# A mixture-of-experts kernel on one core: eight experts run straight through, and only TensorE asks for their sizes

## The chip, the cores and the metric

The kernel runs on one core of one Trainium2 chip. The metric is the device time of one execution in microseconds (us). Three runs of the kernel before gave 909.44, 908.67 and 904.90 us, a median of 908.67 us. In the profile the engines are TensorE (PE for its matrix products, PEld for its loads of a stationary operand), VectorE (DVE), ScalarE (ACT), GpSimd (POOL) and SyncE (SP), which issues most of the transfers. A name with q behind it (POOLq, SPq, PEq) is the engine's sequencer, which reads the program and hands work to the engine.

## What is computed

Three parts in a row, all in float32:

```python
# attention over a window of 64 keys: 4 batches, 8 heads, 576 positions, 64 per head
attn = softmax(where(0 <= i - j < 64, q @ k.T / 8, -1e9)) @ v
x = attn.transpose(0, 2, 1, 3).reshape(2304, 512)
# dense: w_in 512 x 2048, w_out 2048 x 512
x = (relu(x @ w_in) ** 2) @ w_out
# routed: 8 experts, w1 512 x 1024, w2 1024 x 512; each token goes to one expert
logits = x @ w_gate
e = argmax(logits);  g = softmax(logits)[e]
out[token] = g * (relu(x[token] @ w1[e]) @ w2[e])
```

How many of the 2304 tokens fall to an expert is known only when the program runs.

## The kernel before

Each float32 operand of a product is kept as a rounded high half and the remainder (names ending in h and l), and a product is made of three matrix products: high by high, high by low, low by high (`mm3`, L165 to L168). Attention and the dense part run interleaved, 256 tokens at a time, and take the first 540 us. Their order is not touched by the change.

**Before the routed part.** When most tokens are routed, the expert with the most tokens so far is picked, and its first two tiles of 128 tokens are run early (expert number -1, `group_of` from L989), beside the end of the gate. For each token the gate writes its number and its weight into a table in memory (`tab_d`), which is read back as `tab`, expert by expert; the number of tokens left for each expert is in `cnt`.

**The routed part** (L1067 to L1072) goes through the experts 0 to 7 in turn. At an expert, every one of the five engines reads the expert's size from `cnt` into a register (L992) and goes down a tree of comparisons (`either`, L1051) to one of eleven copies of the expert's program, made for 128, 192, 256, 288, 320, ... 512 tokens (`SIZES`, L1065). At the end of that copy it jumps behind all of them. `arm` (L997) is one such copy:

- for up to 128 tokens, `tile_of` (L680): the tokens are the stationary operand, 512 hidden columns stream at once, and the hidden values are transposed again for the second product.
- for more, `group_of` (L728): for each of 8 blocks of 128 hidden columns, `up` streams all the tokens through 4 x 3 products, `relu` (L744) splits the result into halves (ACT the high half, DVE the low half), and `down` multiplies the block before with 512 columns of w2, tile by tile, into the banks `ys`. A last tile of at most 64 tokens puts its two halves side by side (L758 to L761).
- between the blocks the next expert is prepared: `split` (L277) turns an eighth of its weights into halves (two casts on ACT, two subtractions on DVE or POOL by the letters of `TILES`) and starts the load of a further eighth into a ring of seven buffers; `gather_tile` (L927) fetches 128 tokens' rows by POOL; `tokens_in` (L930) transposes them on TensorE and splits them into halves. Only the next expert's first two tiles are brought in ahead; its third and fourth at its own start (L1024).
- `scatter` (L789) scales a tile of results on DVE and writes it to the rows of `out` by POOL. An expert's last tile is scattered only when its copy has been left (L1070), from a buffer of its own.

Expert sizes over 512 would run a loop (`more`, L1039).

The order of the instructions on each engine is that of the code in the routed part (`manual_schedule`, L1067); before it, a scheduler orders DVE, POOL and SP.

Of the kernel before, what the change touches and what calls it, by code (L numbers as in the profile page):

```python
# [11 lines left out]
F32 = mybir.dt.float32  # L12
# [37 lines left out]
def kernel(  # L50
# [26 lines left out]
    SPLIT_AT = {1: (0, 1), 3: (2, 3), 5: (4, 5, 6, 7)}  # L77
# [3 lines left out]
    TILES = "a" * 16, "vvvp" * 4  # L81
    TILE = "vvaaaaavaaaaavaa", "vvvppvvppvvpvppp"
# [33 lines left out]
    nc.vector.memset(zero, 0.0)  # L116
    mask = bpool.tile([P, 2, P], F32, tag="mask", name="mask")
# [26 lines left out]
    cnt = cpool.tile([1, E], I32, tag="cnt", name="cnt")  # L144

# [522 lines left out]
    def early_tokens(t):  # L668
        ps = transposed(early["x"][t]).rearrange("p (k t) -> p k t", k=KD)
        halves(*(x[:, :, ST + t * P:ST + t * P + P] for x in xhl), ps)  # L670
# [52 lines left out]
    def half_tile(n):  # L723
        m = n % P
        return m if m <= P // 2 and n > P else 0


    def group_of(e, n, c0, ys, new_g, between, first=None):  # L728

        h1, l1, h2, l2 = wsp[e]  # L730
        T = -(-n // P)
        m = half_tile(n)
        hid = {}

        def up(f, a, m, ks=range(KD)):

            if f not in hid:
                hid[f] = psum("h", 2)
            xh, xl = (x[:, :, c0 + a:c0 + a + m] for x in xhl)
            for kk in ks:  # L740
                b_ = slice(kk * F1 + f * P, kk * F1 + f * P + P)
                mm3(hid[f][:, a:a + m], h1[:, b_], l1[:, b_], xh[:, kk, :], xl[:, kk, :], kk == 0, kk == KD - 1)

        def relu(f):  # L744
            h, l = new_g()
            ps = hid[f]
            nc.scalar.activation(h[:, :n], ps[:, :n], ACTF.Relu)  # L747
            for o, a in ((l[:, :n - m], slice(n - m)), (h[:, n:n + m], slice(n - m, n)))[:1 + (m > 0)]:
                nc.vector.scalar_tensor_tensor(  # L749
                    out=o, in0=ps[:, a], scalar=0.0, in1=h[:, a].bitcast(F32), op0=ALU.max, op1=ALU.subtract  # L750
                )
            hid[f] = h, l

        def down(f, ts=range(T)):
            gh, gl = hid[f]
            b_ = slice(f * DM, f * DM + DM)
            for t in ts:
                if m and t == T - 1:  # L758
                    a = slice(n - m, n + m)
                    nc.tensor.matmul(ys[t][:2 * m, :], lhsT=gh[:, a], rhs=h2[:, b_], start=f == 0, stop=False)  # L760
                    nc.tensor.matmul(ys[t][:2 * m, :], lhsT=gh[:, a], rhs=l2[:, b_], start=False, stop=f == 7)  # L761
                else:
                    a = slice(t * P, min(t * P + P, n))
                    mm3(ys[t][:a.stop - a.start, :], gh[:, a], gl[:, a], h2[:, b_], l2[:, b_], f == 0, f == 7)

        ts = [T - 1, *range(T - 1)] if m else range(T)
        for f in range(8):
            if f == 0 and T > 2:
                up(f, 0, 2 * P)
                up(f, 2 * P, n - 2 * P)  # L770
            elif f == 0 and first:
                up(f, 0, n, range(KD // 2))
                first()
                up(f, 0, n, range(KD // 2, KD))
            else:
                up(f, 0, n)
            relu(f)
            if f == 7:
                between(f)
            if f:  # L780
                down(f - 1, ts if f < 7 else ts[:2])
            if f < 7:
                between(f)
        down(7, ts[1::-1] if m else ts[:2])
        for t in ts[2:]:
            down(6, (t,))
            down(7, (t,))
# [142 lines left out]
    def tokens_in(t, m=P, x=None, ps=None):  # L930

        if x is None:
            x = xg[t]
        ps = transposed(x, ps).rearrange("p (k t) -> p k t", k=KD)[:, :, :m]
        halves(*(x[:, :, t * P:t * P + m] for x in xhl), ps)
# [16 lines left out]
    def between(f):  # L952
# [3 lines left out]
        if f == 1:  # L956
# [4 lines left out]
            count(cnt, ps)  # L961
            nc.sync.dma_start(tab, tab_d.rearrange("(p r) c -> p r c", p=P))
        if f == 2:
# [4 lines left out]
            early["r"] = rpool.tile([P, 4 * P], F32, tag="r", name="r")  # L968
            early["ylast"] = rpool.tile([P, DM], F32, tag="ylast", name="ylast")
# [19 lines left out]
    group_of(-1, 2 * P, ST, ybanks[2:], new_g, between, first)  # L989
# [5 lines left out]
    rpool, ylast = early["pool"], early["ylast"]  # L995

    def arm(e, n):  # L997

        T = -(-n // P)
        ys = ybanks[:T - 1] + ybanks[3:]  # L1000
        m = half_tile(n)
        if m:
            ys[T - 2], ys[T - 1] = ys[T - 1], ys[T - 2]
        col = e * KMAX

        def between(j):
            if j == 1 and e + 1 < E:
                for k in (2, 3):
                    gather_tile(e + 1, k)
            if j == (4 if T == 1 else 7) and e + 1 < E:  # L1010
                for k in range(2):
                    tokens_in(k, ps=ybanks[k] if T == 1 else None)
                    if e + 2 < E:
                        gather_tile(e + 2, k)
            for i in SPLIT_AT.get(j, ()) if T == 1 else (j,):
                if e + 1 < E:
                    split(e + 1, i, TILE if T == 1 else TILES)

        nc.vector.tensor_copy(lasts[e % 2], tab[:, col + T - 1 - (m > 0), :])  # L1019
        if T == 1:  # L1020
            tile_of(e, 0, ys[0], lambda: early["r"], new_g, between)
        else:
            for t in range(2, T):
                tokens_in(t, min(P, n - t * P))  # L1024
            group_of(e, n, 0, ys, new_g, between)
            T -= m > 0
            for t in range(min(m > 0, T - 1)):
                scatter(ys[t], tab[:, col + t, :], new_r())
            if m:
                y, r = ys[T], new_r()  # L1030
                nc.scalar.copy(r[:m, :], y[m:2 * m, :])
                nc.vector.tensor_tensor(r[:m, :], r[:m, :], y[:m, :], op=ALU.add)
                ent = tab[:m, col + T, :]
                nc.vector.tensor_scalar_mul(r[:m, :], r[:m, :], ent[:, 1:2].bitcast(F32))
                scatter(None, ent, r[:m, :])
            for t in range(m > 0, T - 1):
                scatter(ys[t], tab[:, col + t, :], new_r())

    def more(e, n):  # L1039

        with tc.For_i(4, (n + (P - 1)) // P, 1) as i:
# [5 lines left out]
            tokens_in(2, x=x)  # L1047
# [3 lines left out]
    def either(e, n, sizes):  # L1051

        if len(sizes) == 1:
            arm(e, sizes[0])
            if sizes[0] == 4 * P:
                with tc.If(n > 4 * P):
                    more(e, n)
# [55 lines left out]
```

## Time and profile before

| | |
|---|---|
| median of three runs | 908.67 us (904.90 to 909.44) |
| the profiled execution | 912.93 us |
| its span, from the first to the last instruction | 911.2 us |
| TensorE: products, share of the span | 782.2 us, 86% |
| DVE, ACT, POOL busy | 546.9, 362.8, 311.5 us |
| TensorE's mean granted clock | 0.937 of full speed |

The span runs from 0 to 911.2 us. The early two tiles' last product ends at 578.7 us; there the routed part begins. A product's time in the timeline overlaps the next product's, so the price of one in a row of them is the distance of two starts. The granted clock is given as a share of 2.4 GHz: 0.50 means 1.2 GHz. "issue" in a wait means that the engine waited for nothing the profile shows, as its sequencer had not handed on the next instruction.

### The profile page before, as it was taken

To read this page: it belongs to the slowest core of one execution; us is meant where nothing else is said; L and a number is where in the kernel's file an instruction comes from. 1 tells how busy PE (TensorE), PEld (TensorE's weight loads), DVE (VectorE), ACT (ScalarE), POOL (GpSimd) and SP (SyncE) were. 2 spreads that over 40 slices of the span, in tenths; PEclk is the share of its full clock that TensorE was granted. 3 is DMA by queue.
4 is the path that set the end of the run, shared out by engine and by line. 5 is a ranking of instruction groups with operands and counts; after the bars stand their busy time and mean duration, and the time that the engine had idled before them with its cause. 6 is when DMAs were issued, how large, how long until landed. Compare 5 with 4: busy or idle time off the path is not lost.

```text
span 911.2 us, 14100 instructions
## 1 busy us (share of the span) xinstructions
PE 782.2 (86%) x4995; PEld 680.8 (75%) x4995; DVE 546.9 (60%) x1262; ACT 362.8 (40%) x985; POOL 311.5 (34%) x307
## 2 busy tenths in 40 slices
PE   6977778999999999999999979369446869979795
PEld 5866667888888898888889968258335858868684
DVE  6999995884956648485674966554256243423312
ACT  6845553444444434444443444144134233322200
POOL 5767784122121312222210242553355231221201
PEclk9998999999999999999999999778777698989998
DMA  9635442211202111111110353555365452330101
GB/s 287 224 121 174 140 152 80 71 35 47 68 28 70 47 53 48 41 53 42 59 36 12 123 191 128 191 156 176 116 200 163 145 169 89 119 107 1 46 1 42
DMA packets 49870, 92.24 MB, mean 101 GB/s; under 512 B 7148, under 2 KB 23532, under 8 KB 49680
## 3 DMA queue, kind: packets, MB, share of 16 engines
q1 hardware_dynamic: 44688, 80.43, 27.5%
q0 software_dynamic: 4992, 9.62, 3.4%
q8 instruction: 78, 1.28, 0.7%
q14 instruction: 112, 0.92, 0.4%
HBM read 84.59 MB, written 10.21 MB: 104 GB/s over the span
## 4 chain that ended last, share of the span: by engine, by line
PE 68%; DVE 14%; issue 11%; DMA 3%; ACT 2%; SPq 1%; DVEq 0%; another core or an unknown queue 0%; POOLq 0%; ACTq 0%; POOL 0%
PE h L166 11%; PE h L167 11%; PE h L168 11%; PE y L168 9%; PE y L167 9%; PE y L166 9%; DVE tmp L205 2%; PE a L355 2%; DVE tmp L201 2%; DVE gl L471 2%; DVE tmp L209 2%; PE a L428 2%; PE a L676 2%; DMA vf<-in_v 1%; PE a L413 1%
## 5 line engine op out<-in xcount | busy, mean ns | idle before, releaser
L166 PE MATMUL h<-xh,w 128*128 128x256 f32 (+4 forms) x784 | 241.1, 308 | 9.5 <-DVE last L1019 8.1
L168 PE MATMUL h<-xh,w 128*128 128x256 f32 (+4 forms) x784 | 234.5, 299 | 1.2 <-POOL w L227 1.2
L167 PE MATMUL h<-xl,w 128*128 128x256 f32 (+4 forms) x784 | 235.0, 300 | 0.1
L166 PEld LDWEIGHTS h<-xh,w 128*128 128x128 f32 x784 | 154.8, 198 | 20.5 <-issue 8.5
L167 PEld LDWEIGHTS h<-xl,w 128*128 128x128 f32 x784 | 155.1, 198 | 7.3 <-DVE xl L163 0.5
L168 PEld LDWEIGHTS h<-xh,w 128*128 128x128 f32 x784 | 154.5, 197 | 3.9 <-POOL w L227 1.4
L168 PE MATMUL y<-w,gl 128*128 128x512 f32 x294 | 115.3, 409 | 25.1 <-DVE gl L471 25.1
L457 ACT ACTIVATE r<-h 128x256 f32<-128x256 f32 x144 | 55.3, 384 | 189.3 <-PE h L168 174.2
L166 PE MATMUL y<-w,gh 128*128 128x512 f32 x294 | 117.3, 399 | 0.8 <-ACT gh L464 0.6
L167 PE MATMUL y<-w,gh 128*128 128x512 f32 x294 | 116.5, 396 | 0.0
L466 DVE TENSOR_TENSOR r<-r 128x256 f32<-128x256 f32 x112 | 54.8, 489 | 72.5 <-ACT gh L464 63.5
L749 DVE SCALAR_TENSOR_TENSOR ggl<-h,ggh 128x256 fp32r<-128x256 f32 (+2 forms) x45 | 23.1, 513 | 119.5 <-ACT ggh L747 117.9
L541 DVE SCALAR_TENSOR_TENSOR tmp<-tmp,stg 128x512 f32<-128x512 f32 x128 | 91.4, 714 | 0.7
L275 POOL TENSOR_TENSOR w<-stg,w 128x512 fp32r<-128x512 f32 x35 | 45.9, 1324 | 133.4 <-ACT w L274 115.3
L329 POOL COPY q<-qd 64x256 f32<-64x256 f32 x56 | 46.0, 822 | 126.5 <-PE a L355 121.1
L471 DVE TENSOR_TENSOR gl<-r,gh 128x256 fp32r<-128x256 f32 x144 | 78.0, 542 | 14.7 <-POOL r L466 10.8
L168 PEld LDWEIGHTS y<-w,gl 128*128 128x128 f32 x294 | 53.8, 190 | 40.5 <-DVE gl L471 30.1
L747 ACT ACTIVATE ggh<-h 128x448 fp32r<-128x448 f32 (+3 forms) x45 | 21.6, 480 | 131.8 <-PE h L168 92.5
L166 PEld LDWEIGHTS y<-w,gh 128*128 128x128 f32 x294 | 55.8, 190 | 8.6 <-ACT gh L464 1.4
L464 ACT ACTIVATE gh<-r 128x256 fp32r<-128x256 f32 x144 | 60.0, 418 | 3.7
L227 POOL TENSOR_TENSOR w<-tmp,w 128x512 fp32r<-128x512 f32 x32 | 52.5, 1645 | 24.7 <-ACT w L226 24.5
L407 POOL TENSOR_TENSOR s<-s,tot 128x512 f32<-128x512 f32 x28 | 30.8, 1099 | 88.4 <-DVE tot L406 33.4
(179 smaller groups left out, 1404.3 us busy)
## 6 DMA issues: line engine op xcount, KB each, us to landing
stg<-in_moe_w SPq DMA_DIRECT2D x45, 512.0 KB
stgx<-in_moe_w SPq DMA_DIRECT2D x18, 512.0 KB
stg<-in_moe_w_in SPq DMA_DIRECT2D x16, 512.0 KB
stg<-in_moe_w_out SPq DMA_DIRECT2D x16, 512.0 KB
v<-in_v SPq DMA_DIRECT2D x28, 256.0 KB
x_d<-tmp SPq DMA_DIRECT2D x18, 256.0 KB
q<-in_moe_w SPq DMA_DIRECT2D x9, 512.0 KB
qd<-in_q SPq DMA_DIRECT2D x28, 128.0 KB
```

The lines of the kernel that those rows point to most:

```text
L166: nc.tensor.matmul(o, lhsT=ah, rhs=bh, start=first, stop=False)
L167: nc.tensor.matmul(o, lhsT=ah, rhs=bl, start=False, stop=False)
L168: nc.tensor.matmul(o, lhsT=al, rhs=bh, start=False, stop=last)
L227: nc.gpsimd.tensor_tensor(l, c, h.bitcast(F32), op=ALU.subtract)
L275: rest.tensor_tensor(l[:, a:a + 512], src, h[:, a:a + 512].bitcast(F32), op=ALU.subtract)
L329: nc.gpsimd.tensor_copy(qk[g][rows, :, half, :], d[rows])
L407: nc.gpsimd.tensor_tensor(s, s, tot.unsqueeze(2).to_broadcast([P, HP, P]), op=ALU.mult)
L457: nc.scalar.activation(r, gT[st, f][:, :ST], ACTF.Relu)
L464: nc.scalar.square(gh, r)
L466: sq.tensor_tensor(r, r, r, op=ALU.mult)
L471: nc.vector.tensor_tensor(gl, r, gh.bitcast(F32), op=ALU.subtract)
L541: nc.vector.scalar_tensor_tensor(out=junk, in0=x2sb[tt], scalar=1.0, in1=w, op0=ALU.mult, op1=ALU.mult, accum_out=l[:, t, e:e + 1])
```

## The change

The routed part becomes one straight program for eight experts of four tiles each, whatever their sizes. `either`, `arm`, the eleven sizes, the half tiles and the late scatter of the last tile go. `group` is the one program:

- DVE, ACT, POOL and SP do the work of four tiles for every expert: relu on 512 columns, four tiles gathered, brought in and scattered. Rows of the table that hold no token name a row out of bounds, which the gather and the scatter leave out.
- TensorE alone reads the sizes, all eight in the early group's step 6. In each of an expert's 8 steps it picks a width of 256, 352, 448 or 512 columns for `up` by two comparisons, and for each of the tiles 3, 2 and 1 by one comparison whether `down` runs or a product of 2 columns with zeros stands in its place.
- The next expert's four tiles are brought in during steps 5 and 7, into columns that the running expert doesn't use or has used up (`base` alternates between 256 and 0).
- 6 of 16 subtractions of a split are on POOL, where 4 were; the ring of result buffers has four.
- Sizes over 512 are asked for once, behind all experts, by all engines.

```diff
-    SPLIT_AT = {1: (0, 1), 3: (2, 3), 5: (4, 5, 6, 7)}
+    GROUP = 4 * P
+    WIDTHS = (256, 352, 448, 512)
-    TILES = "a" * 16, "vvvp" * 4
-    TILE = "vvaaaaavaaaaavaa", "vvvppvvppvvpvppp"
+    TILES = "a" * 16, "vvpvvpvpvvpvvpvp"
...
+    pr.make([P, 512], F32, "h", 2)
+    for bank in pr.tiles["h"]:
+        nc.vector.memset(bank[:, 2 * P:], 0.0)
...
+    def group(e, c0, new_g, between, n=None, first=None, after=None):
...
+            def part(m, ks=range(KD)):
+                for kk in ks:
+                    b_ = slice(kk * F1 + f * P, kk * F1 + f * P + P)
+                    xh, xl = (x[:, kk, c0:c0 + m] for x in xhl)
+                    mm3(hid[f][:, :m], h1[:, b_], l1[:, b_], xh, xl, kk == 0, kk == KD - 1)
+
+            def least(sizes):
+                if len(sizes) == 1:
+                    part(sizes[0])
+                    return
+                mid = len(sizes) // 2
+                with tc.If(n > sizes[mid - 1]) as c:
+                    least(sizes[mid:])
+                with c.Else():
+                    least(sizes[:mid])
...
+            for t in reversed(range(width // P)):
+                if n is None or t == 0:
+                    tile_(t)
+                    continue
+                with tc.If(n > t * P) as c:
+                    tile_(t)
+                with c.Else():
+                    nc.tensor.matmul(ys[t][:, :2], lhsT=nil, rhs=nil[:, :2], start=True, stop=True, skip_group_check=True)
...
+    def expert_in(e, ks):
+        for k in ks:
+            tokens_in(xg[k], base(e) + k * P)
+            if e + 1 < E:
+                gather_tile(e + 1, k)
...
         if f == 6:
-            for k in range(2):
-                tokens_in(k)
-            for k in range(2):
-                gather_tile(1, k)
+            ns.extend(
+                nc.values_load(cnt[0:1, e:e + 1], engines={mybir.EngineType.PE}, min_val=0, max_val=NT) for e in range(E)
+            )
+            expert_in(0, range(4))
...
-    ns = [nc.values_load(cnt[0:1, e:e + 1], min_val=0, max_val=NT) for e in range(E)]
...
+            if f == 5:
+                expert_in(e + 1, (0, 1) if base(e + 1) == 0 else (2, 3))
+            if f == 7:
+                expert_in(e + 1, (2, 3) if base(e + 1) == 0 else (0, 1))
+            split(e + 1, f, TILES)
...
     with tc.manual_schedule():
         for e in range(E):
-            if e:
-                scatter(ybanks[3], lasts[(e - 1) % 2], ylast)
-            either(e, ns[e], SIZES)
-        scatter(ybanks[3], lasts[(E - 1) % 2], ylast)
+            group(e, base(e), new_g, next_of(e), n=ns[e])
+            for t in reversed(range(GROUP // P)):
+                scatter(ybanks[t], tab[:, e * KMAX + t, :], new_r())
+        with tc.If(nc.values_load(most[0:1, 0:1], min_val=0, max_val=NT) > GROUP, preferred_fallthrough_block=False):
+            for e in range(E):
+                n = nc.values_load(cnt[0:1, e:e + 1], min_val=0, max_val=NT)
+                with tc.If(n > GROUP):
+                    more(e, n)
```

The first place is TensorE at the end of an expert. Before, from the last products of expert 0's smallest copy (`y` is a bank of results, `w` a unit of weights, `a` a bank for transposes):

```order
L166 MATMUL y_132<-w_700,ggh 128x512
L167 MATMUL y_132<-w_701,ggh 128x512
L168 MATMUL y_132<-w_700,ggl 128x512
L1060 UNCONDITIONAL_BRANCH
L992 TENSOR_LOAD cnt
L1060 COMPARE_AND_BRANCH x4
L676 MATMUL a_208<-ident,k 128x128 x4
```

And now, in `down` of a step: tile 1's comparison, its three products or the small one, tile 0, and the next step's comparisons (`nil` is the tile of zeros):

```order
L786 COMPARE_AND_BRANCH
L171 MATMUL y_135<-w_703,ggh 128x512
L172 MATMUL y_135<-w_704,ggh 128x512
L173 MATMUL y_135<-w_703,ggl 128x512
L786 UNCONDITIONAL_BRANCH
L790 LDWEIGHTS nil
L790 MATMUL y_135<-nil 128x2
L786 UNCONDITIONAL_BRANCH
L171 MATMUL y_134<-w_703,ggh 128x512
L172 MATMUL y_134<-w_704,ggh 128x512
L173 MATMUL y_134<-w_703,ggl 128x512
L751 COMPARE_AND_BRANCH x2
```

One load of a register and a jump between whole copies per expert have become comparisons over a few dozen instructions in every step; a taken path meets nine of them in a step (three for the width, two for each of three tiles).

The second place is DVE at the same point. Before, with the scatter of the last tile, the load of the size, the tree and the first instruction of a copy (`last` is a copy of the last tile's table entry):

```order
L1060 UNCONDITIONAL_BRANCH
L791 TENSOR_SCALAR ylast<-y_132,last_5277 128x512
L992 TENSOR_LOAD cnt
L1060 COMPARE_AND_BRANCH x4
L1019 COPY last_5278<-tab 128x2
```

And now, the four tiles of an expert's results and the next expert's first step:

```order
L805 TENSOR_SCALAR s_1150<-y_137,tab 128x512
L805 TENSOR_SCALAR s_5404<-y_136,tab 128x512
L805 TENSOR_SCALAR s_1148<-y_135,tab 128x512
L805 TENSOR_SCALAR s_1149<-y_134,tab 128x512
L751 UNCONDITIONAL_BRANCH x2
L768 SCALAR_TENSOR_TENSOR ggl<-h_93,ggh 128x512
L280 TENSOR_TENSOR w_702<-stg_156,w_701 128x512
```

DVE loads no size and compares nothing; of TensorE's choices it keeps short unconditional branches from one piece of its program to the next, as ACT, POOL and SP do.

## Rows read from the trace of the kernel before

**Rows 1.** Stretches of the span: stretch, length, busy time of each engine (instructions), clock, DMA.
```profile
core 0: us, PE busy (x) PEld busy (x) DVE busy (x) ACT busy (x) POOL busy (x), PEclk, DMA share, GB/s
578.70:899.90 321.20, 243.94 (x1164) 207.45 (x1164) 120.16 (x208) 90.03 (x176) 97.10 (x87) 0.85 0.36 113
899.90:911.20 11.30, 0.01 (x1) 0.00 (x0) 0.75 (x1) 0.00 (x0) 2.72 (x3) 0.72 0.17 59
```
**Rows 2.** TensorE's waits from 575 us on: in total, times, longest.
```profile
PE h L166 <- issue: 26.3, 2, 13.6
PE a L676 <- issue: 21.1, 4, 8.1
```
**Rows 3.** Stretches again, one around each of the eight experts' products.
```profile
592.30:608.10 15.80, 15.80 (x64) 12.26 (x64) 7.87 (x11) 9.46 (x18) 6.41 (x6) 0.83 0.43 135
616.20:642.30 26.10, 26.05 (x152) 23.60 (x152) 14.38 (x24) 12.39 (x26) 8.62 (x8) 0.90 0.55 176
654.90:673.00 18.10, 15.26 (x64) 11.86 (x64) 10.88 (x14) 9.46 (x18) 10.40 (x9) 0.88 0.50 160
685.00:704.00 19.00, 15.57 (x64) 12.04 (x64) 12.61 (x16) 9.46 (x18) 10.92 (x10) 0.86 0.53 163
708.70:744.00 35.30, 35.30 (x183) 31.54 (x184) 14.71 (x34) 13.42 (x28) 9.05 (x8) 0.83 0.44 144
751.40:797.70 46.30, 44.55 (x212) 38.71 (x212) 17.51 (x36) 15.09 (x29) 10.59 (x10) 0.93 0.33 103
804.20:851.90 47.70, 47.65 (x220) 39.72 (x220) 17.03 (x28) 14.83 (x28) 9.95 (x9) 0.95 0.09 30
856.70:899.90 43.20, 43.20 (x204) 37.37 (x204) 9.11 (x22) 5.92 (x11) 2.09 (x3) 0.96 0.03 11
```
**Rows 4.** Groups by shape from 540 us on: tile, shape, count, busy, mean ns.
```profile
L166 PE MATMUL h<-xh,w 128*128 128x448 f32 x56 | 20.6, 367 | 0.0
L166 PE MATMUL h<-xh,w 128*128 128x480 f32 x28 | 10.7, 382 | 0.0
L166 PE MATMUL h<-xh,w 128*128 128x288 f32 x28 | 9.0, 322 | 0.0
```
**Rows 5.** TensorE's timeline (start, time, instruction, count); last, eight transposes in the chain.
```profile
555.43 0.28 PE L166 MATMUL h<-xh,w 128*128 128x256 f32 x1
...
556.39 0.28 PE L168 MATMUL h<-xh,w 128*128 128x256 f32 x1
556.51 0.39 PE L166 MATMUL y<-w,gh 128*128 128x512 f32 x1
...
557.66 0.40 PE L168 MATMUL y<-w,gl 128*128 128x512 f32 x1
...
616.75 0.41 PE L168 MATMUL h<-xh,w 128*128 128x256 f32 x1
...
791.70 0.87 PE a L676 x8
```
**Rows 6.** Groups by shape from 751 to 850 us, POOL: subtraction of a split, gather.
```profile
L275 POOL TENSOR_TENSOR w<-stg,w 128x512 fp32r<-128x512 f32 x5 | 6.8, 1368 | 41.8 <-ACT w L274 28.4 <-issue 13.4
L922 POOL DMA_INDIRECT k<-x_d,tab x4 | 4.1, 1032 | 7.9 <-PE a L676 7.6 <-issue 0.3
```
**Rows 7.** Timeline where experts 6 and 7 meet, TensorE and DVE, with the idle time before.
```profile
851.46 0.39 PE L168 MATMUL y<-w,ggl 128*96 128x512 f32 x1
...
853.41 0.75 DVE L791 TENSOR_SCALAR ylast<-y,last 128x512 f32<-128x512 f32 x1 [2.13 <-issue]
854.20 0.17 DVE L1019 COPY last<-tab 128x2 int32<-128x2 int32 x1
856.66 1.59 PE L676 MATMUL a<-ident,k 128*128 128x128 f32 x8 [4.81 <-issue]
```
**Rows 8.** DMA queues of the page, one of the two for instructions: packets, MB, share.
```profile
q8 instruction: 78, 1.28, 0.7%
```
**Rows 9.** Timeline at the end: the last scatter.
```profile
903.18 0.97 POOL L792 DMA_INDIRECT out<-ylast,last  x1 [1.23 <-DVE ylast L791]
```

More of the change, by code (lines that the diff above doesn't have):

```diff
@@ L144 @@
     cnt = cpool.tile([1, E], I32, tag="cnt", name="cnt")
+    most = cpool.tile([1, 1], I32, tag="most", name="most")
     x2_d = dpool.tile([NT, DM], F32, tag="x2_d", name="x2_d")
@@ L721, in tile_of, with up @@
         down(1, t1, range(4))
[L723 to L728, printed above, removed]
+    def group(e, c0, new_g, between, n=None, first=None, after=None):
         h1, l1, h2, l2 = wsp[e]
-        T = -(-n // P)
-        m = half_tile(n)
+        ys = ybanks[2:] if n is None else ybanks
+        width = GROUP if n is not None else 2 * P
         hid = {}
[L735 to L742, printed above, removed]
+        def up(f):
+            hid[f] = psum("h", 2)
+            def part(m, ks=range(KD)):
[12 more added lines that the diff above has]
+                    least(sizes[:mid])
+            if n is not None:
+                least(WIDTHS)
+            elif f == 0:
+                part(width, range(KD // 2))
+                first()
+                part(width, range(KD // 2, KD))
+            else:
+                part(width)
@@ L744, in relu @@
         def relu(f):
             h, l = new_g()
[L746 to L751, printed above, removed]
+            nc.scalar.activation(h[:, :width], hid[f][:, :width], ACTF.Relu)
@@ L752, in relu, with down @@
+            nc.vector.scalar_tensor_tensor(
+                out=l[:, :width], in0=hid[f][:, :width], scalar=0.0, in1=h[:, :width].bitcast(F32),
+                op0=ALU.max, op1=ALU.subtract,
+            )
             hid[f] = h, l
-        def down(f, ts=range(T)):
+        def down(f):
             gh, gl = hid[f]
             b_ = slice(f * DM, f * DM + DM)
[L757 to L764, printed above, removed]
@@ L987, in new_g @@
         return [g[:, t, :] for g in early["g"]]
-    group_of(-1, 2 * P, ST, ybanks[2:], new_g, between, first)
+    group(-1, 0, new_g, between, first=first)
     for t in range(2):
         scatter(ybanks[2 + t], early["ent"][:, t, :], new_r())
-    ns = [nc.values_load(cnt[0:1, e:e + 1], min_val=0, max_val=NT) for e in range(E)]
     done.pop("gather")
     order.__exit__(None, None, None)
[L995 to L1037, printed above, removed]
@@ L1039, in more, with next_of, between @@
-    def more(e, n):
-        with tc.For_i(4, (n + (P - 1)) // P, 1) as i:
+    rpool, nil = early["pool"], early["nil"]
+    def next_of(e):
+        def between(f):
+            if e + 1 == E:
+                return
+            if f == 5:
[3 more added lines that the diff above has]
+            split(e + 1, f, TILES)
+        return between
+    def more(e, n):
+        wsp.pop(e)
+        for i in range(8):
+            wload(e, i)
+            wsplit(e, i, TILES)
+        with tc.For_i(GROUP // P, (n + (P - 1)) // P, 1) as i:
```

57 lines of the change are left out of this document (19 added, 38 removed).

## The prediction, made before the result was known

> **What bounds the kernel now.** I read the stretches of the span first. The routed part lasts from 578.7 to 899.9 us, 321.2 us, and TensorE is busy for 243.9 of them [rows 1]; no other engine is busy for half of it. So 77.3 us are idle time of the engine that has most to do. TensorE's waits say why: the largest entries are "issue", two gaps of 26.3 us together, the longest 13.6, and four more of 21.1 us [rows 2]. The reader is to see that no transfer and no engine is named there: TensorE's sequencer had no next instruction to hand on, and that happens where one expert ends and the next copy of the program is looked for.
>
> Then I read the stretches of the single experts [rows 3]. Three experts have 64 matrix instructions, which is the copy for up to 128 tokens (24 up, 24 down, 16 transposes); the others can be told by the shapes of their products [rows 4]: one of 288 columns, two of 448, one of 480; the remaining one, the second, has 152 instructions (96, 48 and 8), so two tiles, 256 columns. The counts of [rows 4] are of 28 for an expert, as the first block is cut in two. In the new program these sizes take the widths 256 (four experts), 352, 448, 512 and 448, and 1, 2, 1, 1, 3, 4, 4, 4 tiles. None is over 512, so the loop for more isn't run.
>
> The clock is the third thing to see. It is below 1 in every expert's stretch. Length times the missing share gives 2.7 + 2.6 + 2.2 + 2.7 + 6.0 + 3.2 + 2.4 + 1.7 = 23.5 us [rows 3]. The expert that begins at 616.2 us, after a gap, has products of 256 columns of 0.41 us where they take 0.28 at full clock [rows 5]: it starts at 1.2 GHz, half speed. So the gaps cost these 23.5 us once more. At full clock its work in the routed part is 243.9 - 23.5 = 220.4 us.
>
> **The change, part by part.** All sums are against the profiled execution, 912.93 us with a span of 911.2, so 1.7 us lie around the span. The median of the three runs is 908.67, 0.5% less; the predicted time is scaled to it at the end.
>
> *Removed: the gaps.* 77.3 us of idle time and 23.5 us of slow clock, 100.8 us, are what there is to gain if TensorE is never without an instruction.
>
> *Added: work of TensorE.* At full clock, products of 256 columns start 0.12 us apart (8 steps in 0.96 us) and those of 512 columns 0.23 us apart (5 steps in 1.15 us); eight transposes take 0.87 us [rows 5]. Between the two, by a straight line, I take 0.16 us for 352 and 0.20 for 448 columns. An expert has 96 products in `up`, 24 for each tile in `down`, and 16 transposes for the next expert (1.7 us; the last has none). Small expert: 96 x 0.12 + 24 x 0.23 + 1.7 = 18.7 us, three times 56.2. Second: 11.5 + 11.0 + 1.7 = 24.3. Fifth: 15.4 + 16.6 + 1.7 = 33.7. Sixth: 19.2 + 22.1 + 1.7 = 43.0. Seventh: 22.1 + 22.1 + 1.7 = 45.9. Last: 41.3. Together 244.4 us, 24 more than the 220.4 of now: a small expert streams 256 columns where at most 128 hold tokens, and the half tiles are gone. The 96 small products with zeros have no row; above, they cost no more than a transpose each (0.11 us, 10 us in all), below nothing; I take 3.
>
> *Moved: the other engines do four tiles for every expert.* The sixth expert does that already: DVE 17.5, ACT 15.1 us busy [rows 3]. DVE gives two subtractions to POOL. POOL then has 6 x 1.37 for the split and eight gathers and scatters of 1.03 us, 16.4 us [rows 6]. So a small expert has 18.7 us of TensorE beside 17, 15 and 16 us of three engines that work in order and wait for each other. The cover is thin there, and I add 4 us to each of the three; for the other five, with 24 us and more of TensorE, 0.8 us each where experts meet (the next expert's last two tiles are split on ACT and DVE in step 7, behind the relu that the last products wait for). Together 16 us; bounds 0 and 40. DVE's four scalings at an expert's start stand in front of the next relu; TensorE has two blocks of `up` to do meanwhile, 2.9 us against four times 0.75 [rows 5, 7].
>
> *Added: 576 branches on TensorE*, nine in each of 64 steps. Whether they lie on the path is the unknown that matters. The nearest rows: where experts 6 and 7 meet, DVE's scaling starts at 853.41 and its next instruction at 854.20, and in these 0.79 us its sequencer loaded a size, made three comparisons and took a jump [rows 7]; the scaling itself took 0.75, so the next one started without an idle gap. At most that is 0.2 us each, 115 us in all; below it is nothing, as for DVE here, and not less. For TensorE: the start of the first expert takes three far jumps and has the gap of 13.6 us [rows 2], 4.5 us a jump; where experts 6 and 7 meet it takes two (out of the copy for 480, into the one for 448), and the gap is 4.81 us [rows 7]. The other 4 us passed under products that were already handed on. So TensorE's sequencer reads ahead of its products, and I take nothing for the branches. That cover is gone where TensorE waits with nothing queued; the 16 us above include it.
>
> [...]
>
> *Added: code for TensorE is skipped in small jumps.* A step's program holds four widths, of which one runs. The instruction queue's packets are 1.28 MB / 78 = 16 KB [rows 8]. No row shows a short jump on TensorE. A far one costs 4.5 us; below, a jump within what is loaded costs nothing. I take nothing, and keep the other end for a rival.
>
> *Start and end.* The early group brings in four tiles where it brought in two, 0.9 us of transposes, which must wait for ACT and DVE between the two pairs, and TensorE loads eight sizes: at most 8 x 0.79 us by DVE's bound, at least nothing. I take 4 us together, bounds 0 and 9. At the end, TensorE's last product was followed by 11.3 us [rows 1]; the last scatter's issue starts at 903.18, takes 0.97, and the span ends 7.0 us after it [rows 9]. Now no jump stands between the last product and the last scaling: 0.75 + 0.97 + 7.0 = 8.8 us, and I take 10 for the question about sizes over 512.
>
> *Sum.* 578.7 + 4 + 244.4 + 3 + 16 + 10 = 856.1 us of span, 857.8 with what lies around it, 55 us less than 912.93. Scaled by 908.67/912.93: 854 us.
>
> **The rivals.**
>
> *The small experts are held by the other engines.* For: three engines within 4 us of TensorE, each in program order, so one late cast holds the rest. Against: their busy times are below TensorE's. If each of the first four experts took 28 us in place of 22.7 and 25 us, 19 us would be added: 873 us.
>
> *TensorE pays for its branches.* For: they are its own, in every step, and no row shows short ones. Against: rows 7. At 0.08 us each on the path, 576 x 0.08 = 46 us: 900 us. [...]
>
> *TensorE waits for its code.* This is the one that ends slower. Place: every step in which a jump leads out of what has been loaded. Price: 4.5 us each, the far jump's [rows 2]. It decides from 55 / 4.5 = 12 of the 64 steps on; in half of the steps it would add 144 us: 998. For: the old gaps are of just this kind. Against: the jumps skip a few dozen instructions, and code in a row has been streaming without waits in the products of [rows 5]. [...]
>
> **How the numbers follow.** The forecast (838 to 870) has 0.70, the held small experts 0.13 (865 to 885), the paid branches 0.07 (885 to 920), the code 0.10 (above 890, mostly above 915). The low end: without waits, without a dearer start and with the short end, 578.7 + 244.4 + 8.8 + 1.7 = 833.6, scaled 830, all bounds at once; 838 leaves some 0.05 below. The upper end takes in the held experts and half of the paid branches: 895. Within 0.5%, about what a measurement here can tell from no change, is 904 to 913: a part of the branches' and of the code's cases, 0.04. Slower: 0.11. Faster: 0.85.
>
> **What would show it.** Right: TensorE's "issue" waits in the routed part fall from some 77 us to a few; the clock there stays near 1; a small expert lasts 21 to 25 us, start to start, the seventh about 47; the routed part lasts about 264 us. The engines' rival: TensorE's waits name DVE, ACT or POOL in the first four experts. The branches: even gaps under 1 us at each step, in the large experts too. The code: "issue" gaps of some us, scattered over the steps. The prediction is wrong if the routed part lasts over 290 us, or if TensorE's products at full clock sum to far more than 244 us.

## The result and the profile after

The changed kernel takes 871.68 us (median of four runs, 871.15 to 872.83) where the one before took 908.16 beside it; the ratio is 0.9605, with an interval of 0.9577 to 0.9633. The forecast was 854, so the gain is 36 us where 55 were expected. The profiled execution took 872.06 us, its span is 870.3, and TensorE's mean granted clock 0.977.

The three stretches that answer to [rows 1] are the last of the early group's products after 578.70, the eight experts, and the tail. The columns are those of [rows 1].

```profile
578.70:582.04 3.34, 3.34 (x18) 3.08 (x18) 1.74 (x4) 1.68 (x4) 1.51 (x2) 0.77 0.36 132
582.04:850.15 268.11, 260.48 (x1463) 223.64 (x1461) 152.38 (x196) 110.03 (x205) 116.50 (x98) 0.99 0.40 128
850.15:870.30 20.15, 0.00 (x1) 0.00 (x0) 0.79 (x2) 0.00 (x0) 2.93 (x3) 0.58 0.13 46
```

The routed part went from 321.2 us to 271.45 (3.34 + 268.11), at a clock of 0.99 in place of 0.85. The tail grew from 11.3 to 20.15 us. These two lines are the result: some 50 us won, 9 given back, 41 us of the span. The medians show 36, as the profiled execution of the kernel before took 912.93 us, 4.8 more than the median beside the changed kernel.

TensorE's waits from 570 us on, beside [rows 2]:

```profile
PE a L681 <- issue: 2.8, 1, 2.8
PE y L790 <- DVE s L805: 2.6, 5, 1.1
PE y L173 <- DVE ggl L768: 1.5, 2, 0.8
PE y L171 <- DVE s L805: 1.1, 2, 0.5
PE a L681 <- DVE xl L168: 1.0, 1, 1.0
PE y L790 <- issue: 0.8, 3, 0.4
```

The far jumps between the experts are gone; one "issue" gap of 2.8 us is left, with five short ones of 1.3 us in all, and now DVE is named in most lines. The single experts, beside [rows 3], each from its first product of `up` to the next one's:

```profile
582.04:607.60 25.56, 22.81 (x167) 19.89 (x166) 18.44 (x24) 15.24 (x29) 14.70 (x13) 1.00 0.52 167
607.60:635.15 27.55, 27.42 (x177) 24.23 (x177) 20.75 (x28) 14.96 (x28) 17.70 (x15) 0.94 0.55 169
635.15:658.05 22.90, 21.42 (x161) 18.57 (x159) 20.89 (x26) 14.96 (x28) 15.27 (x14) 1.00 0.74 232
658.05:682.65 24.60, 21.71 (x160) 18.83 (x161) 23.14 (x26) 14.86 (x28) 17.59 (x16) 1.00 0.61 187
682.65:718.27 35.62, 35.23 (x194) 30.71 (x193) 22.30 (x32) 15.08 (x28) 18.69 (x16) 1.00 0.57 188
718.27:761.98 43.71, 43.71 (x210) 37.77 (x209) 20.00 (x27) 15.07 (x28) 16.29 (x15) 1.00 0.42 133
761.98:808.00 46.02, 46.02 (x209) 37.72 (x208) 18.32 (x27) 15.08 (x28) 12.18 (x11) 1.00 0.12 43
808.00:850.15 42.15, 42.15 (x193) 35.91 (x191) 8.54 (x13) 4.79 (x8) 4.09 (x5) 1.00 0.07 24
```

In the last three TensorE is busy all the time. In the small ones (first, third, fourth) it isn't, and in the fourth DVE is busy longer than TensorE (23.14 and 21.71 us). The second starts at a granted clock of 0.50 (607.6 to 610.9 us): its products of 256 columns last 0.41 us until 610.9, and 0.28 from 611.05 on, after two small gaps of TensorE (0.77 and 0.35 us, which end at 605.7 and 606.8 us). At 0.50 these products start 0.214 us apart, 1.2 columns a nanosecond; the profile gives the clock as a share alone, so 1.2 GHz for 0.50 is an estimate from such starts, if a column takes one clock.

### The profile page after: what moved, and what is told of

It reads as the page before. It is cut to its first block, busy times and chain, and to the rows that moved or that the text cites. A ratio compares the mean times of both kernels' runs of the same rounds, so it can differ in the third digit from the quotient of the medians.

```text
span 870.3 us, 15066 instructions
## 1 busy us (share of the span) xinstructions
PE 800.3 (92%) x5295; PEld 699.6 (80%) x5295; DVE 579.7 (67%) x1253; ACT 383.5 (44%) x1015; POOL 334.5 (38%) x324
## 5 line engine op out<-in xcount | busy, mean ns | idle before, releaser
L171 PE MATMUL h<-xh,w 128*128 128x256 f32 (+3 forms) x864 | 263.5, 305 | 1.2 <-ACT r L462 0.7
L172 PE MATMUL h<-xl,w 128*128 128x256 f32 (+3 forms) x864 | 257.3, 298 | 0.7 <-DVE xl L168 0.4
L173 PE MATMUL h<-xh,w 128*128 128x256 f32 (+3 forms) x864 | 257.3, 298 | 0.4 <-POOL w L232 0.4
L171 PEld LDWEIGHTS h<-xh,w 128*128 128x128 f32 x864 | 166.7, 193 | 13.2 <-issue 2.0
L172 PEld LDWEIGHTS h<-xl,w 128*128 128x128 f32 x864 | 166.9, 193 | 9.2 <-DVE xl L168 1.1
L173 PEld LDWEIGHTS h<-xh,w 128*128 128x128 f32 x864 | 166.5, 193 | 4.2 <-POOL w L232 0.7
L173 PE MATMUL y<-w,gl 128*128 128x512 f32 x294 | 114.7, 407 | 26.1 <-DVE gl L476 25.6
L768 DVE SCALAR_TENSOR_TENSOR ggl<-h,ggh 128x512 fp32r<-128x512 f32 (+1 forms) x69 | 46.0, 667 | 102.2 <-ACT ggh L767 97.5
L767 ACT ACTIVATE ggh<-h 128x512 fp32r<-128x512 f32 (+1 forms) x69 | 40.3, 584 | 149.6 <-PE h L173 114.4
L471 DVE TENSOR_TENSOR r<-r 128x256 f32<-128x256 f32 x112 | 50.8, 454 | 72.3 <-ACT gh L469 72.0
L476 DVE TENSOR_TENSOR gl<-r,gh 128x256 fp32r<-128x256 f32 x144 | 81.9, 569 | 14.7 <-POOL r L471 10.9
L171 PE MATMUL y<-w,ggh 128*128 128x512 f32 x170 | 70.4, 414 | 1.1 <-DVE s L805 1.1
L173 PE MATMUL y<-w,ggl 128*128 128x512 f32 x170 | 67.7, 398 | 1.6 <-DVE ggl L768 1.5
L172 PE MATMUL y<-w,ggh 128*128 128x512 f32 x170 | 66.8, 393 | 0.0
```

The costliest lines, as they stand in the source:

```text
L171: nc.tensor.matmul(o, lhsT=ah, rhs=bh, start=first, stop=False)
L172: nc.tensor.matmul(o, lhsT=ah, rhs=bl, start=False, stop=False)
L173: nc.tensor.matmul(o, lhsT=al, rhs=bh, start=False, stop=last)
L471: sq.tensor_tensor(r, r, r, op=ALU.mult)
L476: nc.vector.tensor_tensor(gl, r, gh.bitcast(F32), op=ALU.subtract)
L767: nc.scalar.activation(h[:, :width], hid[f][:, :width], ACTF.Relu)
```

## The experiments

Each is told by its edit of the changed kernel, if nothing else is said. Ratios are to the kernel before, measured beside each. Its median there lay between 907.0 and 910.0 us, so a difference of less than some 3 us between the times of two experiments is not shown by the times alone. The lengths of stretches are from the profiled execution of each.

**1. Was what there was to gain sized rightly?** The kernel before, with each expert's copy chosen at build time:

```diff
-            either(e, ns[e], SIZES)
+            arm(e, (128, 256, 128, 128, 288, 448, 480, 448)[e])
```

> The kernel before with the copy for every expert fixed when the program is built (128, 256, 128, 128, 288, 448, 480, 448 tokens): the same products, no size is loaded and no engine takes a branch. It leaves out the choice at run time. Theory: the gaps between the experts are the code looked for behind far jumps, 77.3 us of idle time and 23.5 us of slow clock; without them the small experts (16 us of TensorE) are held by the split of the next expert's weights on DVE, ACT and POOL at about 20 us, so some 10 to 20 us of the 100.8 come back as waits on those engines: 820 to 835. Rival: the gaps come from the waits for the next expert's weights and tokens and only show as issue; then the time stays over 880.

It took 826.94 us, ratio 0.9109 (0.9055 to 0.9163). Its stretch of the eight experts, which answers to the first line of [rows 1]:

```profile
578.70:814.20 235.50, 222.84 (x1152) 189.95 (x1150) 127.65 (x201) 88.07 (x174) 99.17 (x85) 0.98 0.43 145
```

85.7 of the 321.2 us went with the questions. The gaps were what bounded the kernel, and the clock was theirs too: 0.98 instead of 0.85, and 222.84 us of TensorE where 220.4 had been worked out at full clock. The other 15 of the 100.8 us are mostly waits that the gaps had covered (7.5 and 4.0 us for DVE's `xl` and `ggl` are the largest). So the change could not have won 100, and by its shape it gives back more: wider products, and all engines at four tiles.

**2. Do the branches on TensorE cost time?** Widths and tiles fixed at build time, no branch left, the small products and the eight loads kept:

```diff
-                with tc.If(n > t * P) as c:
+                if n > t * P:
...
-            group(e, base(e), new_g, next_of(e), n=ns[e])
+            group(e, base(e), new_g, next_of(e), n=(128, 256, 128, 128, 288, 448, 480, 448)[e])
```

> The changed kernel with every expert's width and tiles fixed when the program is built, to what the sizes of this input choose, the small products with zeros included: TensorE issues the same products in the same order and takes none of the 576 branches; the other engines lose their short branches. It leaves out the choice at run time; TensorE still loads the eight sizes. Theory: TensorE's sequencer reads ahead and the branches are hidden; its waits named issue in the routed part are 1.3 us in all; the time is within 3 us of 871.7. Rival: the branches cost 0.02 to 0.08 us each on TensorE or hold the engines beside it, and 12 to 46 us go: 826 to 860.

It took 865.84 us, ratio 0.9537 (0.9478 to 0.9596): 5.8 us less, between the two theories. Where the 5.8 us are tells more. The last four experts, first the changed kernel, then this one:

```profile
682.65:850.15 167.50, 167.11 (x801) 142.11 (x800) 69.16 (x96) 50.01 (x92) 51.24 (x44) 1.00 0.28 93
```
```profile
677.13:844.65 167.52, 166.98 (x801) 142.10 (x799) 69.24 (x96) 49.98 (x92) 51.19 (x45) 1.00 0.29 92
```

The branches of these 32 steps, nine in each, cost nothing at all. Undisturbed steps of small experts last 2.30 us in both. The 5.5 us by which the last product comes sooner lie ahead of 677 us: 1.7 in the early group's last step, 2.1 in the first small expert and 1.9 in the third and fourth, where TensorE also waits for DVE. Whether a branch adds there what it can't hide, or the steps of DVE only fall differently, no run separates.

**3. What does the question at the end cost?** First the kernel without it, without the reduction into `most`, and without `more`:

```diff
-        with tc.If(nc.values_load(most[0:1, 0:1], min_val=0, max_val=NT) > GROUP, preferred_fallthrough_block=False):
-            for e in range(E):
...
```

> The changed kernel without the question about sizes over 512 behind the last expert (and without the loop that it guards; the maximum of the sizes isn't taken either). In the changed kernel 20.2 us lie between TensorE's last product and the end of the span, 11.3 in the kernel before. Theory A: the question holds POOL. Its row of events shows the last scatter's issue ending at 853.9, waits until 857.6, a counter step of 1.9 us, a compare-and-branch at 859.6 and the closing drain of 7.3 us only from 862.2 on; without the question the drain starts right behind the last scatter's issue and the time falls by 8 us, to 863 to 865. Rival B: the four scatters at the very end and their landing make the tail long; then the time stays within 2 us of 871.7.

It took 862.69 us, ratio 0.9493 (0.9436 to 0.955), 9.0 less than the changed kernel. Its tail, from TensorE's last product on, against the 20.15 above:

```profile
848.70:860.50 11.80, 0.00 (x0) 0.00 (x0) 0.79 (x2) 0.00 (x0) 2.92 (x3) 0.61 0.19 74
```

What POOL's sequencer does there in the changed kernel (columns: line, instruction, count, least, median and longest ns, first and last start):

```profile
L1053 POOLq EVENT_SEMAPHORE  x6: 17/30/43, 851.7 to 857.6; - x6
...
L1053 POOLq COMPARE_BRANCH  x2: 40/40/41, 851.6 to 859.6; - x2
...
L1053 POOLq INC_SWDGE_SEM  x1: 1919/1919/1919, 857.7 to 857.7; - x1
...
L1094 POOLq DRAIN  x3: 40/112/7259, 862.2 to 870.0; - x3
```

and in the run without the question:

```profile
L1088 POOLq DRAIN  x3: 40/113/10126, 849.5 to 860.2; - x3
```

The program ends with a drain of POOL. Without the question it starts at 849.5 us, while the scatters are still being issued, and covers them. With it, POOL goes through semaphores until 857.6, raises a counter for 1.9 us, jumps, and only then, at 862.2, begins a drain that again takes 7.26 us. The question lays one wait behind another.

Then the question before the last expert, with a free part of `xhl` and the free weight tiles for `more`:

```diff
+            if e == E - 1:
+                units = wsp[E - 2]
+                with tc.If(nc.values_load(most[0:1, 0:1], min_val=0, max_val=NT) > GROUP, preferred_fallthrough_block=False):
+                    for e_ in range(E):
...
```

> The changed kernel with the question, and the loop behind it, moved from behind the last expert to ahead of it. Theory A (the question holds POOL's way to the closing drain): the tail shrinks by 8 us as without the question. TensorE now takes the jump over the loop's code (3.3 us at the end of the changed kernel) between the seventh and the last expert. If it reads ahead there, under the seventh expert's last products, it pays 0 to 2 us, and the time is 864 to 866; if it pays the jump in full and starts again at 1.2 GHz, 3.3 + 2 us, and the time is 868 to 870. Rival B (the landing of the last scatters): no gain at the end, 872 to 877.

It took 869.82 us, ratio 0.956 (0.9502 to 0.9619). The tail is 11.78 us, but TensorE now pays:

```profile
PE h L171 <- issue: 4.5, 1, 4.5
```

and the last expert starts slow after that gap: its first products of 448 columns last 0.58 us, where the mean of [rows 4] is 0.37 (43.88 us for the expert instead of 42.15). It is the far jump of [rows 2] once more, at the 4.5 us that the prediction took for one. So a third form: the same place, and in the question one loop over the experts in place of eight copies of `more`:

```diff
-                    for e_ in range(E):
-                        n = nc.values_load(cnt[0:1, e_:e_ + 1], min_val=0, max_val=NT)
+                    with tc.For_i(0, E, 1) as e_:
+                        n = nc.values_load(cnt[0:1, ds(e_, 1)], min_val=0, max_val=NT)
```

> The question about sizes over 512 stands before the last expert, as in the run that took 869.8, and the code that it skips is one loop over the experts in place of eight copies. Theory A: the 4.5 us for which TensorE waited there are the fetch of code that lies far away; over a body of an eighth of the length the jump costs under 1 us, and the time is 865 to 867. Rival: the price is that of any question which all engines ask, whatever the length that is skipped: 869 to 871, and TensorE's issue wait there is again about 4.5 us.

It took 865.84 us, ratio 0.9522 (0.9488 to 0.9557). TensorE's wait there:

```profile
PE h L171 <- PEq L1060: 1.1, 1, 1.1
```

1.1 us in place of 4.5, a little over what Theory A had. So the price of this question on TensorE fell with the length of the code that it skips; these two lengths are all that was tried.

**4. The eight loads.** One size is loaded in the early group, each further one in step 3 of the expert before:

```diff
-            ns.extend(
-                nc.values_load(cnt[0:1, e:e + 1], engines={mybir.EngineType.PE}, min_val=0, max_val=NT) for e in range(E)
-            )
+            size_of(0)
...
+            if f == 3:
+                size_of(e + 1)
```

> TensorE's eight size loads, in a row in the early group's step 6 in the changed kernel, are spread: the first stays, each further one is loaded in step 3 of the expert before. Theory A: the eight loads (0.30 us each) are what TensorE waited for in its one gap of 2.83 us (at 574.65), which is followed by 1.2 GHz until about 580; a single load lies under products already handed on. Then the gap goes and the clock stays up: 868 to 869.5 against 871.7. Rival: each load holds TensorE by itself wherever it stands, 0.3 us of gap in each expert, so nothing is won: 871 to 873.

It took 868.38 us, ratio 0.9572 (0.9531 to 0.9613), 3.3 less, which the times alone don't show: its four runs lie between 866.8 and 872.8 us, and the profiled one is the shortest. In that trace the "issue" gap of 2.8 us is gone, though TensorE now waits 2.9 us for DVE's `xl` where it waited 1.0, and every expert ends 2.5 to 3.8 us sooner. The clock did not stay up, as Theory A had it: products of 256 columns last 0.41 us after the new wait too, from 575.8 to 577.5 us. So the trace has the place from the first theory, the eight loads, and only a part of its account.

**5. What holds the small experts?** First the split's subtractions as in most copies of the kernel before, twelve on DVE and four on POOL (its copy for up to 128 tokens had eight on POOL, by the string `TILE`):

```diff
-    TILES = "a" * 16, "vvpvvpvpvvpvvpvp"
+    TILES = "a" * 16, "vvvp" * 4
```

> The changed kernel with the split's subtractions as before the change: twelve on DVE and four on POOL for an expert, in place of ten and six. Theory A: a subtraction on POOL lengthens those on DVE beside it (DVE's mean is 1.04 to 1.22 us in the changed kernel, 0.68 in the large experts of before), so that two fewer on POOL cost DVE nothing in sum: its busy time in a small expert stays at 18 to 23 us and the time is 866 to 870. Rival: DVE is what small experts wait for, and two more subtractions of 0.68 us add 1.4 us to each of the four: 874 to 878. If TensorE alone sets the pace: 871 to 873.

It took 861.46 us, ratio 0.9479 (0.9449 to 0.9508): 10.2 us less, for one string, and more than either theory had. Then two that tell the number from the order: `"vvvpvpvpvvvpvpvp"`, six on POOL and none first in its pair, and `"v" * 16`, none on POOL.

> The changed kernel with six subtractions of an expert's split on POOL, as before, but each the second of its pair (vv vp vp vp vv vp vp vp; in the changed kernel the third and eleventh stand first in their pair, pv). It asks whether the 10 us that were won with four on POOL come from their number or from which of them start beside one of DVE's. Theory A, the start beside each other: DVE's mean for a subtraction falls from 1.04-1.13 us to 0.80 or less, and the time to 861 to 865. Rival, the number on POOL: DVE's mean stays over 0.95, and the time is 868 to 872.

> The changed kernel with all sixteen subtractions of the split on DVE, none on POOL. Theory A: the collision with POOL is what DVE's subtractions lose; without it each takes 0.68 to 0.70 us, sixteen take 11 us for an expert (12 x 0.72 = 8.7 in the run with four on POOL), and since DVE isn't full the time stays at 859 to 864. Rival: DVE's work in program order is what small experts wait for, and 2.5 us more for each of the first five add 8 to 12 us to the 861.5 of the run with four on POOL: 869 to 874.

They took 866.06 (ratio 0.9559, 0.9523 to 0.9596) and 863.09 us (0.953, 0.9494 to 0.9566); the second comes out as its Theory A had it. Their profiled executions are the longest of their five, 872.25 and 868.36 us, so that only the means of single instructions are taken from them. DVE's subtractions from the tile `stg`, between 582 and 840 us (count | busy, mean ns of one), in the changed kernel, with four on POOL and with none:

```profile
L280 DVE TENSOR_TENSOR w<-stg,w 128x512 fp32r<-128x512 f32 x41 | 42.6, 1054 | 1.7 <-ACT w L279 1.6
```
```profile
L280 DVE TENSOR_TENSOR w<-stg,w 128x512 fp32r<-128x512 f32 x49 | 35.3, 746 | 0.1
```
```profile
L280 DVE TENSOR_TENSOR w<-stg,w 128x512 fp32r<-128x512 f32 x66 | 42.4, 683 | 0.1
```

DVE is busy for 42.6 us with 41 subtractions, and for 42.4 us with 66. What POOL took over, DVE lost in longer ones. One place of the changed kernel shows how (timeline of POOL and DVE):

```profile
627.77 1.02 POOL L936 DMA_INDIRECT k<-x_d,tab  x1 [0.31 <-issue]
628.32 3.60 DVE L280 TENSOR_TENSOR w<-stg,w 128x512 fp32r<-128x512 f32 x1 [0.24 <-ACT w L279]
628.81 2.55 POOL L280 TENSOR_TENSOR w<-stg,w 128x512 fp32r<-128x512 f32 x2
```

DVE's subtraction of 0.68 us ends half a microsecond after POOL's two do: by these times it all but stood still beside them. POOL's gathers and scatters don't do that, since in the run with none on POOL the mean is 0.683 with all of them there. Nor does it happen to DVE's other subtraction, of the relu, which has one of its two inputs in PSUM: in the changed kernel and with none on POOL it takes the same.

```profile
L768 DVE SCALAR_TENSOR_TENSOR ggl<-h,ggh 128x512 fp32r<-128x512 f32 x63 | 43.2, 686 | 90.9 <-ACT ggh L767 90.8
```
```profile
L768 DVE SCALAR_TENSOR_TENSOR ggl<-h,ggh 128x512 fp32r<-128x512 f32 x63 | 43.5, 690 | 88.3 <-ACT ggh L767 88.3
```

So the subtraction with both inputs in SBUF takes 1054 ns with six of sixteen on POOL and 683 with none, the one with an input in PSUM 686 and 690. Whether the place of the inputs makes that difference, no run separates. With six behind DVE's (the second run) the mean is 0.82 to 0.96 us, by tile, and about half of the 10 us are won: by these means order and number both count, and neither theory of that run holds alone.

**6. And the four tiles for every expert?** The kernel of experiment 2, with every engine at the tiles that an expert has and no small products:

```diff
-        width = GROUP if n is not None else 2 * P
+        width = -(-n // P) * P if n is not None else 2 * P
...
-            for t in reversed(range(GROUP // P)):
+            for t in reversed(range(-(-SZ[e] // P))):
```

> The kernel with the sizes known at build time (865.8) once more, and now every engine handles the tiles that an expert has instead of four: gathers, transposes, casts, relu, scatters for 1, 2, 1, 1, 3, 4, 4, 4 tiles; no small products with zeros. The products of up keep their widths. Theory A: the four tiles for every expert are what makes a small expert last 22 to 28 us where TensorE's products take 18.7; they fall to 17.5 to 20 and the time to 848 to 856 (TensorE also saves 12 x 0.87 us of transposes, 10 us of it). Rival: the split of the next expert's weights, which stays, is what they wait for; then only part of the transposes' time is won: 857 to 864.

It took 844.17 us, ratio 0.9302 (0.9267 to 0.9338), 21.7 less than experiment 2 and 4 below the range of Theory A, which had the small experts right. (Its text takes 0.87 us for a tile's transposes; that is the price of two tiles', [rows 5], so at most 5 of the 21.7 are theirs.) The third and fourth expert last 19.06 and 18.98 us instead of 22.30 and 23.32. An undisturbed step of a small expert lasts 2.13 us, 12 x 0.12 + 3 x 0.23 as predicted, where it lasts 2.30 with three small products. So of the 21.7 us some 5 are transposes and 6.4 the small products (the next section has their sum), both TensorE's own work; the other 10 are what waits and start gave back, by subtraction.

**7. The edits that won, together.** Four on POOL, the loads apart, and the question in short code before the last expert:

> Three edits that won alone, together: four subtractions on POOL (-10.2 us), a size loaded for each expert apart (-3.3), and the question before the last expert over one loop of code (-5.8). If the three hold at different places, they add: 871.7 - 19.3 = 852.4, 850 to 855. Rival: the first two both win in the first small expert, where what is won at its start is then lost to DVE: 855 to 859.

It took 853.07 us, ratio 0.9423 (0.9388 to 0.9459): the three add up. It asks all that the changed kernel asks. Its tail is 11.83 us, its experts last 260.49 (with the early group's last six products) at a clock of 1.00:

```profile
577.98:838.47 260.49, 256.79 (x1463) 221.25 (x1461) 139.11 (x210) 109.79 (x205) 97.02 (x84) 1.00 0.40 133
```

On top of it TensorE was let off the transposes of tiles that an expert doesn't have:

```diff
+            with tc.If(more_than[0] > more_than[1]) as cc:
+                transposed(x, ps)
```

> The run with three edits (853.1), and TensorE also skips the four transposes of a tile that an expert doesn't have: 9 tiles of the second to fifth expert, 36 transposes of 0.11 us, 3.9 us, against 9 more small products with zeros of some 0.1 us. Theory A: with DVE's subtractions no longer stretched, TensorE's own work sets the small experts, so what it is spared is won: 849.5 to 851. Rival: the small experts still wait for DVE and ACT, which cast these tiles all the same: 852.5 to 854.

It took 854.76 us, ratio 0.9408 (0.9377 to 0.9438); nothing was won, as the rival had it (0.8 us above its range). TensorE still waits for DVE's `s` and `ggl` at the small experts' ends.

## Why the prediction was right, and where its sum was off

The direction and the mechanism hold. The gaps went (TensorE's idle time in the routed part fell from 77.3 to 7.6 us), and the clock came back (0.85 to 0.99) as the second half of the gain; experiment 1 shows both with one edit.

One reading behind this was too short. [rows 2] has 47.4 us of waits named "issue", not 77: the other lines of the same stretch name DVE, 29.9 us.

```profile
PE h L166 <- DVE w L274: 14.8, 1, 14.8
PE h L166 <- DVE last L1019: 8.1, 1, 8.1
PE a L676 <- DVE last L1019: 7.0, 1, 7.0
```

They are the same jumps. Before each of the three DVE had itself stood at "issue", for 10.25, 3.78 and 4.64 us. Around the longest, the 14.8 us before 685 us, the three comparisons that TensorE's sequencer made took 4.4 to 6.3 us each:

```profile
683.95 0.17 DVE L1019 COPY last<-tab 128x2 int32<-128x2 int32 x1 [10.25 <-issue]
```
```profile
L1060 PEldq COMPARE_BRANCH  x3: 4437/5967/6254, 668.0 to 678.8; - x3
```

So DVE too paid for far jumps in the kernel before, and the 0.79 us of [rows 7], taken where experts 6 and 7 meet, are no bound for these three places. Experiment 1 settles it: without the questions 12.7 us of TensorE's waits are left in the routed part, all of them for DVE's `xl` and `ggl`.

Of the rivals two did not come: TensorE was hardly ever without code inside the steps (its waits named "issue" in the routed part sum to 1.3 us), and the branches cost nothing in 32 steps and at most 5.8 us in all (experiment 2). The 0.08 us that the prediction took for each branch in this rival, half of them in its bound of 895, no run shows: 5.8 us over 576 branches are 0.01 us each. The third, the small experts held by the other engines, came in part: TensorE's waits name DVE there, as its sign had it, and experiment 5 shows DVE's subtractions as what held them, but at 22.9 to 25.6 us they stayed under the 28 of its price. The time, 17.7 us too low and 1.7 above the forecast's upper end of 870, goes back to three steps of the sum.

**The tail, "I take 10 for the question about sizes over 512": 20.15, so 10.2 too low.** This step failed in its mechanism. I read the 7.0 us behind the last scatter of before [rows 9] as a fixed end and added 1.2 us for the question, for which no row stands. In the trace the 7.0 us are POOL's drain, and the question moves its start: 8.35 us between the tails with and without it (20.15 and 11.80), 9.0 by the medians, where 1.2 were taken. The trace of before had a row for a part of it, POOL's counter steps at the questions (the last section has it). The other 3 us stand in the 11.80: four scatters in a row on POOL, 1.28 us from one to the next, so that the last starts 2.1 us later than the one I counted, and an end 8.0 us after it instead of 7.0.

**The routed part, 4 too low.** The sum has TensorE's last product at 846.1; it was at 850.15. The length of a step in which TensorE doesn't wait gives where. "The 96 small products with zeros; I take 3": 0.17 us for three of them (2.30 against 2.13), 0.15 for two, 0.14 for one, so 24 x 0.17 + 8 x 0.15 + 8 x 0.14 = 6.4, that is 3.4 too low, within its bounds of 0 and 10. The three last experts, 131.9 us against 130.2: 1.7 too low, by the straight lines for 448 columns. The start, 4 taken and 4.7 measured (3.34 us to 582.04, and 1.4 us for six products of the early group that stand behind it). The waits, 16 taken: 25.56 - 1.4, 22.90 and 24.60 against 8 x 2.30 + 1.74 = 20.1 are 4.1, 2.8 and 4.5; the second expert, with steps of 2.97, has 2.0 (1.65 of it slow clock, 27.55 x 0.06), and the fifth, with steps of 4.11, has 1.0: 14.4 together. So the term's size was right, but by luck, as what it was made of wasn't: I held three engines with little slack to be the cause, and it was mostly DVE, stretched by the very subtractions that POOL took from it (with four on POOL the third and fourth expert last 21.0 and 21.7 us). In the prediction that move stands as relief, without a bound for what it does to DVE. The trace of before had a row for one: in its routed part, where the copy for up to 128 tokens gives POOL eight subtractions of sixteen, DVE's took 0.957 us on average, and 0.683 from 751 us on, where POOL has four:

```profile
L275 DVE TENSOR_TENSOR w<-stg,w 128x512 fp32r<-128x512 f32 x41 | 38.4, 957 | 10.6 <-ACT w L274 8.7 <-issue 1.4
```

**The scaling, 3.8 us.** I took the profiled execution of before to be 0.5% slow and scaled all by it. The changed kernel's runs lie within 1.7 us of each other, its profiled one among them, so there the scaling took off time that was real. Why the runs of the kernel before lie further apart, no trace here shows.

## What to carry to other kernels

A question that all engines ask shows on each of them in another way: price it on the engine that ends last, and see whether it stands in front of a wait that until then lay under other work. Where TensorE had products queued, its short branches were free (167.50 us for four experts with them, 167.52 without); where it jumped over a long piece of code, making that piece a loop took the wait from 4.5 to 1.1 us. When the largest waits name no engine, read the lines below them too, and what the engine that they name waited for. Before work is handed to POOL, compare DVE's mean for the same instruction with and without POOL busy: six subtractions of sixteen taken off DVE that make the other ten half as long again (1054 in place of 683 ns) are no relief.

## What was not expected of the chip

TensorE's own branches span a wide range. In the changed kernel, beside `down`:

```profile
L786 PEldq COMPARE_BRANCH  x288: 65/176/2410, 583.5 to 846.8; - x144
```

and at the questions of the kernel before:

```profile
L1060 PEldq COMPARE_BRANCH  x31: 65/3738/6254, 578.1 to 896.3; - x31
...
L1060 POOLq COMPARE_BRANCH  x31: 34/45/53, 581.3 to 901.9; - x31
L1060 POOLq INC_SWDGE_SEM  x12: 818/1090/1662, 611.2 to 900.2; - x12
```

So half of the far ones took 3.7 us or more on TensorE. On the other engines the records of the same 31 are short, 0.03 to 0.07 us each, but that is not the jump's price there: on DVE the time stands behind the record, as in the 10.25 us of "issue" before 683.95 above. POOL also paid for its questions with counter steps of about 1.1 us. By these rows TensorE's near ones have a median of 176 ns, its far ones one of 3.7 us. The near ones are not seen in the time where products are queued (experiment 2); of the far ones 4.5 us were left over in experiment 3.

Two more things had not been expected: a subtraction on DVE that takes 3.60 us instead of 0.68 while POOL subtracts; and a granted clock that fell to 0.50 for some 3 us after gaps of only 0.77 and 0.35 us (second expert), and is 1.00 for the whole routed part in experiment 7.
